# Spectral filter beside an MLP: the forward width transform as ten times 64 on VectorE and five full blocks on TensorE, filter loads behind the tile transposes, new instruction order

## The chip, the cores and the metric

The kernel runs on one core of one Trainium2 chip. The metric is device time in microseconds (us). Five engines work side by side, each with an instruction stream of its own: TensorE (PE, matmuls), VectorE (DVE), ScalarE (ACT), GpSimd (POOL) and SyncE (SP, which here issues most DMAs). They meet only at semaphores.

## The reference

The sum of three things: the input, a two-dimensional spectral filter of its normalized rows, and a two-layer MLP of the same normalized rows. S is 2048, D is 640, F is 1536, all in bf16.

```python
def _A_ref(x, w_r, w_i):
    B, S, D = x.shape
    X = jnp.fft.rfft2(x.astype(jnp.float32), axes=(-2, -1))
    X = X * (w_r + 1j * w_i)
    return jnp.fft.irfft2(X, s=(S, D), axes=(-2, -1)).astype(jnp.bfloat16)

def _B_ref(x, w1, b1, w2, b2):
    h = _gelu(jnp.einsum("bsd,df->bsf", x, w1) + b1)
    return jnp.einsum("bsf,fd->bsd", h, w2) + b2

xn = _layernorm(x, axis=-1)
return x + _A_ref(xn, A_w_r, A_w_i) + _B_ref(xn, B_w1, B_b1, B_w2, B_b2)
```

## The kernel before

**Tiles.** The 2048 rows are 16 tiles c of 128 rows (row 16p + c lies on partition p); two tiles that follow each other are a pair. Each tile is loaded into `X`, its statistics are taken on DVE (L670, L672), the inverse deviation on POOL (L674, `rstd`), and the normalized tile is written to `T` on DVE (L695).

**The MLP.** Normalized tiles are transposed into `xnT`: tiles 0 to 3 on PE (L714), 4 to 15 by DMA transposes that SP issues (L702). The first layer multiplies `xnT` with the first weights (in the profile `ps<-xnT,W`), ACT applies the gelu into `gT` (L774), and the second layer multiplies `gT` with the second weights (`ps<-W,gT`: a 512-column and a 128-column matmul, a pair, for each 128 of F and each tile). For the tiles in `KEEP` the second layer is finished early, and DVE adds it to a float32 tile (L948) that already holds the second bias (ACT, L924) and the input x, which a POOL DMA accumulates onto it (L942).

**The spectral branch.** Real transforms, in steps:
- *Folding.* DVE folds a tile's 640 columns twice by symmetry (L726: sums and differences of columns d and 639 - d; L730: the same again), a pair at a time. Four sets of 160 columns come out: four blocks of 128, and one block of 128 made of the four leftovers of 32.
- *First height step.* Each of the five blocks is multiplied with `gtab` (L737), ten matmuls a pair, and copied to `XV` (L742).
- *Forward width transform.* `XV` is multiplied with `etab` (L798). For the tiles of a group, each of four sets takes one matmul with 128 rows and one more with the 32 leftover rows (`width`, L778, gives the two lists; `five` starts and stops the sums). ACT and DVE copy the result into `Xb` (L805), two instructions for a group.
- *Second height step* on `mtab` (L816), four 32 x 32 blocks side by side; the result goes to `Y`.
- *Filter.* DVE multiplies with the filter `Wf` (L841) and adds up (L845) into `Z`.
- *Back.* `ntab` (L850), copies (L861), DMA transposes into `XV` (L866), then `getab` (L888), unfolding on DVE (L896, L901) and `htab` (L954), which adds into the PSUM tile of the MLP's second layer. DVE adds x and the bias (L957), and SP stores (L960).

**What sets the order.** `ORDER` (L158) fixes by numbers which operation follows which on each engine; an engine takes its list strictly from the front. `Sched` puts the semaphore waits where data or a buffer's reuse demands them. PE's list mixes spectral steps with matmuls of the MLP, which need nothing from the spectral branch and fill the time. The queue on SP is such a list too: a transpose that waits for DVE holds all loads behind it.

In the profile most helpers' instructions carry the helper's line: matmuls L550, copies L561 on ACT and L562 on DVE, loads L545.

Of the kernel before, what the change touches and what calls it, by code (L numbers as in the profile page):

```python
# [13 lines left out]
D = 640  # L14
# [13 lines left out]
def _tables():  # L28
# [22 lines left out]
    T["E"] = np.concatenate([e[:128] for e in E] + [np.concatenate([e[128:] for e in E])], axis=1)  # L51
# [50 lines left out]
def dve_us(n, rate=1.0):  # L102
    return 0.066 + n / 960.0 / rate
# [20 lines left out]
class Pool:  # L124
# [52 lines left out]
466 460 463 744 454 448 451 760 457 584 735 769 672 611 647 646 682 683 719 755""",  # L177
    "dve": """0 58 57 59 61 62 63 115 116 121 120 66 65 125 67 70 69 137 71 127 126 140 128 130 131 129 144 143 74 76 73 77 75 78
# [12 lines left out]
LAND = {8: 3.13, 13: 3.63, 14: 5.8, 15: 8.08, 16: 9.04, 18: 11.01, 19: 10.03, 20: 14.89, 21: 11.84, 22: 12.65, 23: 17.41, 26: 18.61, 27: 15.54, 28: 19.46, 30: 16.42}  # L191
LATE = {17: 0.5, 24: 0.4, 25: 0.7, 29: 2.0, 31: 1.0, 33: 0.5, 34: 1.6, 35: 1.4, 37: 1.4, 38: 0.4, 39: 1.7, 40: 2.3, 41: 1.7, 42: 0.2, 43: 0.4, 44: 2.5, 45: 0.4, 46: 2.2, 47: 0.9, 48: 1.6, 49: 2.9, 50: 0.3, 51: 1.2, 52: 2.5, 155: 0.3, 168: 0.9, 179: 1.0, 181: 1.0, 192: 0.6, 205: 1.0, 219: 0.7, 591: 1.1}
# [277 lines left out]
def bass_parallel_sum__spectral_gfnet__dense_activation_gelu__prompt_kernel(  # L470
# [21 lines left out]
    with ExitStack() as es:  # L492
# [14 lines left out]
        etab = sb("etab", [128, 800])  # L507
# [25 lines left out]
        XN, X1, XF = 0, 4 * D, 6 * D  # L533
# [7 lines left out]
        p_xn, p_x1, p_xf, p_xb, p_y, p_t, p_z, p_u = Pool(2), Pool(1), Pool(2), Pool(2), Pool(2), Pool(2), Pool(2), Pool(3)  # L541
# [42 lines left out]
        B_g, B_e, B_m, B_n, B_ge, B_h, B_w2 = [Buf(x) for x in ("g", "e", "m", "n", "i", "h", "w2")]  # L584
# [45 lines left out]
        def load_w2(h, **kw):  # L630
            load(W2[:, 3 * h:3 * h + 3, :], w2v[:, 3 * h:3 * h + 3, :], B_w2, (24, 1280), **kw)
# [12 lines left out]
        load(etab[:], const["E"], B_e, (8, 1600), gate=turned[3])  # L644
# [19 lines left out]
        for c0, n in [(c, 1) for c in range(4)] + [(c, 2) for c in range(4, 16, 2)]:  # L664
# [12 lines left out]
        for pair in range(8):  # L677
            xn, x1, xf = Buf(f"xn{pair}", p_xn), Buf(f"xe{pair}", p_x1), Buf(f"xf{pair}", p_xf)

            def xnv(n, o, dims, xn=xn):  # L680
                return view(TT, XN + xn.slot * 2 * D + n * D + o, dims)

            def x1v(o, dims, x1=x1):
                return view(TT, X1 + x1.slot * 2 * D + o, dims)

            def xfv(o, dims, xf=xf):
                return view(TT, XF + xf.slot * 2 * D + o, dims)
            for n in range(2):
                c = 2 * pair + n
                pr = 100 - c / 2  # L690
                B_xn = Buf(f"xn_{c}")
                cuts = (0, 256, D) if not c else (0, D)
                B_xs = [Buf(f"xn_{c}") for _ in cuts[2:]] + [B_xn]
                for d0, d1, bx in zip(cuts, cuts[1:], B_xs):
                    o = K.op([("dve", 0.066 + (d1 - d0) / 1980.0)], pr, lambda e, _, c=c, n=n, xnv=xnv, d0=d0, d1=d1: e.tensor_scalar(  # L695
# [304 lines left out]
```

## Time and profile before

| what | us |
|---|---|
| median of 3 runs | 146.87 |
| lowest and highest | 146.20 and 147.34 |
| span of the profiled execution, first to last instruction | 144.9 |
| first `gtab` run, first `etab` run, first `getab` run start | 15.3, 43.6, 110.1 |
| PE, DVE, ACT busy | 141.2, 112.2, 79.5 |

The profiled execution's own time outside its span is not recorded; the span stands 2.0 us below the median. In a group of the profile, the columns are line, engine, operation, what is written from what, shape and count; then busy us and the mean of one in ns; then the idle time of the engine before them and what ended it. A timeline row is start and length in us, engine, line, operation, count, and in brackets the idle time before it with what ended it. A row of the busy time by stretch gives the stretch, its length, the busy us of PE, PE's weight loads, DVE, ACT and POOL with their counts, the granted clock of PE, the share of the DMA engines and GB/s.

### The profile page before, as it was taken

How to read it: one execution, taken by the hardware profiler on the slowest of the kernel's cores; microseconds unless marked ns; L12 is line 12 of the kernel's file. 1: busy time of each engine (PE TensorE's matmuls, PEld its weight loads, DVE VectorE, ACT ScalarE, POOL GpSimd, SP SyncE). 2: the span in 40 equal slices, each digit the busy share in tenths (PEclk: the TensorE clock that was granted, in tenths of full speed). 3: DMA queues.
4: the chain of work that ended last, by engine and by line, in shares of the span. 5: the costliest groups of instructions: out<-in, count | busy, mean ns of one | idle time of the engine just before them, and what ended most of it. 6: DMA issues, size and time to landing. Idle time of an engine off the chain costs nothing.

```text
span 144.9 us, 4085 instructions
## 1 busy us (share of the span) xinstructions
PE 141.2 (97%) x1720; PEld 90.6 (63%) x1720; DVE 112.2 (77%) x235; ACT 79.5 (55%) x145; POOL 23.8 (16%) x40
## 2 busy tenths in 40 slices
PE   7899999999999999999999999999999999999994
PEld 7799998987455464457554645554446666656573
DVE  1999999999843459799866967992432998998984
ACT  3219999999989668762455633216376755201000
POOL 2331302206100018220200120000054700000000
DMA  4998998987999736948767561362459895103225
GB/s 117 340 410 321 339 164 255 160 146 202 212 301 168 186 59 129 241 104 170 153 179 127 59 144 42 46 142 59 91 112 216 180 209 187 52 5 136 93 106 165
DMA packets 30841, 23.63 MB, mean 163 GB/s; under 512 B 20456, under 2 KB 26856, under 8 KB 30696
## 3 DMA queue, kind: packets, MB, share of 16 engines
q1 hardware_dynamic: 28432, 17.81, 50.5%
q0 software_dynamic: 2368, 5.57, 17.7%
q8 instruction: 13, 0.21, 0.6%
q14 instruction: 4, 0.03, 0.1%
q10 hardware_dynamic: 24, 0.00, 0.0%
HBM read 13.54 MB, written 2.62 MB: 112 GB/s over the span
## 4 chain that ended last, share of the span: by engine, by line
PE 94%; DMA 2%; DVE 2%; issue 0%; ACT 0%
PE ps L550 94%; DMA X<-in_A_x_dram 2%; DVE stats L670 1%; PE ps L714 1%; DVE mv L672 0%; ACT xnT L561 0%; DVE W L957 0%; DVE T L695 0%
## 5 line engine op out<-in xcount | busy, mean ns | idle before, releaser
L550 PE MATMUL ps<-W,gT 128*128 128x512 bf16 (+3 forms) x396 | 58.7, 295 | 0.0
L550 PE MATMUL ps<-xnT,W 128*128 128x256 bf16 (+2 forms) x384 | 58.4, 300 | 0.1
L550 PEld LDWEIGHTS ps<-W,gT 128*128 128x128 bf16 x396 | 30.3, 98 | 23.5 <-issue 1.6
L550 PEld LDWEIGHTS ps<-xnT,W 128*128 128x128 bf16 x384 | 33.3, 98 | 15.7 <-issue 1.6
L774 ACT ACTIVATE gT<-ps,b1col 128x256 bf16<-128x256 f32 (+1 forms) x72 | 35.4, 558 | 6.9 <-PE ps L550 6.5
L670 DVE BATCH_NORM_STATS2 stats<-X 128x6 f32<-128x320 bf16 x32 | 13.9, 476 | 2.1 <-DMA X<-in_A_x_dram 2.1
L561 ACT ACTIVATE Wf<-ps 128x960 bf16<-128x960 f32 (+1 forms) x8 | 7.0, 901 | 13.5 <-PE ps L550 13.5
L942 POOL DMA_DIRECT2D X<-in_A_x_dram x8 | 7.1, 1100 | 39.7 <-DMA Wf<-in_A_w_r_dram 17.1
L841 DVE TENSOR_TENSOR T<-Y,Wf 128x1288 bf16<-128x1288 bf16 x16 | 12.7, 826 | 0.0
L942 POOL DMA_DIRECT2D xnT<-in_A_x_dram x8 | 7.6, 1193 | 25.1 <-ACT xnT L924 25.1
L674 POOL TENSOR_TENSOR rstd<-mv,mhalf 128x2 f32<-128x2 f32 (+1 forms) x10 | 7.1, 714 | 26.6 <-DVE mv L672 26.4
L562 DVE CAST Y<-ps 128x644 bf16<-128x644 f32 x8 | 6.5, 828 | 5.5 <-PE ps L550 5.5
L561 ACT ACTIVATE Xb<-ps 128x960 bf16<-128x960 f32 (+1 forms) x7 | 6.0, 857 | 7.3 <-PE ps L550 7.3
L561 ACT ACTIVATE XV<-ps 128x1280 bf16<-128x1280 f32 (+3 forms) x10 | 9.5, 963 | 0.7 <-PE ps L550 0.7
L562 DVE CAST Xb<-ps 128x960 bf16<-128x960 f32 (+1 forms) x5 | 5.5, 1092 | 4.3 <-PE ps L550 4.2
L730 DVE TENSOR_TENSOR T<-T 128x512 bf16<-128x512 bf16 (+1 forms) x32 | 8.5, 312 | 0.0
L695 DVE TENSOR_SCALAR T<-X,mv,rstd 128x640 bf16<-128x640 bf16 (+2 forms) x17 | 7.1, 430 | 0.9 <-POOL rstd L674 0.6
L896 DVE TENSOR_TENSOR Wf<-Wf 128x960 bf16<-128x960 bf16 (+1 forms) x12 | 7.0, 597 | 0.5 <-ACT Wf L561 0.3
L957 DVE TENSOR_TENSOR W<-ps,X 128x640 bf16<-128x640 f32 x8 | 6.5, 820 | 1.1 <-PE ps L550 1.1
L561 ACT ACTIVATE U<-ps 128x512 bf16<-128x512 f32 (+1 forms) x10 | 3.8, 434 | 6.2 <-PE ps L550 6.2
L845 DVE TENSOR_TENSOR Z<-T 128x644 bf16<-128x644 bf16 x16 | 7.2, 489 | 0.1
L957 DVE TENSOR_TENSOR W<-ps,xnT 128x640 bf16<-128x640 f32 (+2 forms) x10 | 6.7, 686 | 0.7 <-PE ps L550 0.7
(55 smaller groups left out, 135.4 us busy)
## 6 DMA issues: line engine op xcount, KB each, us to landing
X<-in_A_x_dram POOLq DMA_DIRECT2D x8, 320.0 KB, 5.2
xnT<-in_A_x_dram POOLq DMA_DIRECT2D x8, 320.0 KB, 5.1
out_dram<-W SPq DMA_DIRECT2D x15, 160.0 KB, 1.8
X<-in_A_x_dram SPq DMA_DIRECT2D x7, 320.0 KB, 6.7
W<-in_B_w_dram SPq DMA_DIRECT2D x5, 384.0 KB, 5.2
W<-in_B_w_dram SPq DMA_DIRECT2D x4, 480.0 KB, 7.2
Wf<-in_A_w_i_dram SPq DMA_DIRECT2D x6, 160.5 KB, 5.4
Wf<-in_A_w_r_dram SPq DMA_DIRECT2D x6, 160.5 KB, 4.0
```

The lines of the kernel that those rows point to most:

```text
L550: ins = e.matmul(o_, lhsT=lw, rhs=rh, start=st, stop=sp_, skip_group_check=True)
L561: return e.activation(dst(), src(), ACT.Copy, scale=scale)
L562: return e.tensor_copy(dst(), src())
L670: st_op[c] = K.op([("dve", 0.393)], pr, lambda e, _, c=c, h=h: e.bn_stats(stats[:, c, 6 * h:6 * h + 6], view(X, c * D + H2 * h, [[1, H2]]) ...
L674: K.op([("pool", 0.65)], 500, lambda e, _, a=a, b=b: e.tensor_tensor(out=rstd[:, a:b], in0=mv[:, a:b, 1], in1=mhalf[:, a:b], op=ALU.pow), ...
L695: o = K.op([("dve", 0.066 + (d1 - d0) / 1980.0)], pr, lambda e, _, c=c, n=n, xnv=xnv, d0=d0, d1=d1: e.tensor_scalar(out=xnv(n, d0, [[1, d1 ...
L730: ring_ops.append(K.op([("dve", dve_us(4 * w, 2))], pr, lambda e, _, op=op, x1v=x1v, xfv=xfv, o_=o_, o0=o0, o1=o1, w=w: e.tensor_tensor(ou ...
L774: K.op([("act", act_us(128 * nt, 1))], pr + PRIO["gelu"] + GP[bi], lambda e, _, c0=c0, nt=nt, fc=fc, hps=hps, at=at: e.activation(gT[:, fc ...
L841: filt_ops.append(K.op([("dve", dve_us(4 * KP, 2))], pr, lambda e, _, k=k, Y=Y, TB=TB, pair=pair: e.tensor_tensor(out=view(TT, TB.slot * 8 ...
L845: K.op([("dve", dve_us(2 * KP, 2))], pr, lambda e, _, TB=TB, Z=Z, r=r, op=op: e.tensor_tensor(out=view(Zb, Z.slot * 4 * KP + r * KP, [[2 * ...
L942: xo_ops[c] = K.op([("pool", 0.9)], 51 - c / 20, lambda e, _, c=c, xov=xov: e.dma_start(xov(0, D), xv[:, c, :], accum_op=ALU.add), reads=[ ...
L957: K.op([("dve", dve_us(w))], 95, lambda e, _, os_=os_, fps=fps, o0=o0, w=w, xov=xov, base=base: e.tensor_tensor(out=view(W1, OST + os_.slo ...
```

## The change

The forward width transform is cut in another way. 640 is ten times 64: column d is written as 64j + r, and a ten-point real transform over j is made on DVE, four tiles (a quad) at a time, with fourteen instructions: two and three-way sums and differences of columns 320 apart, then the five-point sums with their constants, three of them `scalar_tensor_tensor` (multiply by a constant and add) and one multiplication by a constant. Each tile then has five blocks of 128 columns, which go through `gtab` as before. The `etab` step needs one matmul of 128 rows and 128 columns for each block, and no leftover rows: 80 matmuls in place of 128. The copies into `Xb` then have to spread the results ten or five columns apart, and are four, or three, or two instructions in place of one.

```diff
-        for pair in range(8):
-            xn, x1, xf = Buf(f"xn{pair}", p_xn), Buf(f"xe{pair}", p_x1), Buf(f"xf{pair}", p_xf)
+        for quad in range(4):
+            xn, x1, tm, xf = Buf(f"xn{quad}", p_xn), Buf(f"xe{quad}", p_x1), Buf(f"xs{quad}", p_tm), Buf(f"xf{quad}", p_xf)
...
-            for k, op in enumerate((ALU.add, ALU.subtract)):
-                K.op([("dve", dve_us(640, 2))], pr, lambda e, _, k=k, op=op, xnv=xnv, x1v=x1v: e.tensor_tensor(
...
+            def tt(op, out, in0, in1):
+                return lambda e, _: e.tensor_tensor(out=out(), in0=in0(), in1=in1(), op=op)
+
+            def stt(c_, out, in0, in1):
+                return lambda e, _: e.scalar_tensor_tensor(out=out(), in0=in0(), scalar=c_, in1=in1(), op0=ALU.mult, op1=ALU.add)
...
+            b0 = fold("fp", dve_us(4 * H2, 2), tt(ALU.add, lambda: uv_(0, [[D, 4], [1, H2]]), ...
+            b1 = fold("fm", dve_us(768, 2), tt(ALU.subtract, ...
+            b2 = fold("fn", dve_us(512, 2), tt(ALU.subtract, ...
+            b3 = fold("fs", dve_us(1024, 2), tt(ALU.add, ...
+            b4 = fold("fd", dve_us(1024, 2), tt(ALU.subtract, ...
+            b5 = fold("gs", dve_us(512, 2), tt(ALU.add, ...
+            fold("i1", dve_us(512), stt(kap, ...
+            b6 = fold("gd", dve_us(512, 2), tt(ALU.subtract, ...
+            b7 = fold("ge", dve_us(512), stt(-0.25, ...
+            fold("i2", dve_us(512), stt(-kap, ...
+            b8 = fold("gk", dve_us(512, 2), lambda e, _: e.tensor_scalar(...
+            fold("zr", dve_us(512, 2), tt(ALU.add, ...
+            fold("zp", dve_us(512, 2), tt(ALU.add, ...
+            fold("zm", dve_us(512, 2), tt(ALU.subtract, ...
...
-            pb_ops.append(pe(five_segs(n), PRIO["pb"] - c0 / 10, lambda c0=c0, n=n, bps=bps: five(
-                bps.slot, n, lambda i, g, p0, k: part(XV, p0, k, 2048 * g + 128 * (c0 + i), [[1, 128]]), etab),
+            pb_ops.append(pe([("128", 5 * n * mm_us(128))], PRIO["pb"] - c0 / 10, lambda c0=c0, n=n, bps=bps: [
+                (psb(bps.slot + (g if g < 4 else i), [[1, 128]], 128 * i if g < 4 else 384), view(XV, 2048 * g + 128 * (c0 + i), [[1, 128]]), etab[:, 128 * g:128 * g + 128], True, True)
+                for g in range(5) for i in range(n)],
...
+                    for h in range(2):
+                        k0, dk = (2 * m + 1, 1) if not h else (9 - 2 * m, -1)
+                        ins = copy(lambda: view(xb3, xb.slot * 6 * KP + k0, [[KP, 2 * n], [dk, 2], [10, 32]]),
+                                   lambda: psb(bps.slot + 2 * m, [[64, 2 * n], [512, 2], [1, 32]], 32 * h))(e, name)
+                    for i in range(2 * m, 2 * m + na):
+                        ins = copy(lambda: view(xb3, xb.slot * 6 * KP + 2 * KP * i, [[KP + 5, 2], [5, 64]]),
+                                   lambda: psb(bps.slot + i, [[64, 2], [1, 64]], 384))(e, name)
```

Around it: `rstd` is made tile by tile for eight tiles in place of four; each quarter of the second weights `W2` has a wait of its own; early PSUM tiles of the MLP may use all eight banks (`ZONE["early"]`); the loads that accumulate x no longer wait for the filter loads, and those of the tiles in `SOON` not for the tile transposes either.

```diff
+SOON = (0, 2, 3, 5)
...
-            load(W2[:, 3 * h:3 * h + 3, :], w2v[:, 3 * h:3 * h + 3, :], B_w2, (24, 1280), **kw)
+            load(W2[:, 3 * h:3 * h + 3, :], w2v[:, 3 * h:3 * h + 3, :], B_w2[h], (24, 1280), **kw)
...
-            xo_ops[c].gate += [WL[-1], TD[15]]
-            xo_ops[c].deps += WL + list(TD.values())
+            xo_ops[c].deps += list(TD.values()) if c not in SOON else []
...
 ORDER = {
-    "sp": """8 13 14 17 15 16 19 18 21 22 20 27 30 23 26 28 153 155 166 168 31 32 35 46 48 37 179 181 192 194 38 39 41 34 44 33
+    "sp": """8 13 14 17 15 16 19 18 21 22 27 23 157 159 161 163 28 26 20 31 29 185 187 189 191 30 32 33 35 34 213 217 219 215 46 48
```

All five lists of `ORDER` are new. Rows of the order give the line, the operation, what is written from what, and the written shape; line numbers of the changed kernel are its own.

On DVE, the folding in the first third of the program, before (tile statistics L670 and L672, normalization L695, folds L726 and L730):

```order
L695 TENSOR_SCALAR T<-X,mv,rstd 128x640
L730 TENSOR_TENSOR T<-T 128x2x2x128 x2
L730 TENSOR_TENSOR T<-T 128x2x2x32 x2
L726 TENSOR_TENSOR T<-T 128x2x320 x2
L670 BN_STATS stats<-X 128x6 x4
L672 BN_AGGR mv<-stats 128x2 x2
```

and now the fold of the first quad (sums L752, multiply and add L755, multiplication L770; normalization is L712):

```order
L712 TENSOR_SCALAR T<-X,mv,rstd 128x640 x4
L752 TENSOR_TENSOR T<-Z 128x1024
L752 TENSOR_TENSOR U2<-Z 128x1024
L752 TENSOR_TENSOR T<-T 128x512
L755 SCALAR_TENSOR_TENSOR Y<-U2 128x8x64
L752 TENSOR_TENSOR T<-T 128x8x64
L755 SCALAR_TENSOR_TENSOR Y<-U2 128x8x64
L755 SCALAR_TENSOR_TENSOR T<-T,Z 128x8x64
L770 TENSOR_SCALAR T<-T 128x8x64
L752 TENSOR_TENSOR Y<-T,Z 128x512
L752 TENSOR_TENSOR Y<-T 128x8x64 x2
```

Where a few short folds stood between statistics, eleven of a quad's fourteen instructions now stand in a row, writing the five blocks to `Y`.

On PE, from the last `gtab` runs to the first `etab` runs, before (W1 and W2 are the two weights):

```order
L550 MATMUL ps<-gtab,T 128x64x2 x10
L550 MATMUL ps<-xnT,W1 128x512 x8
L550 MATMUL ps<-gtab,T 128x64x2 x10
L550 MATMUL ps<-xnT,W1 128x512 x6
L550 MATMUL ps<-etab,XV 128x160 x24
L550 MATMUL ps<-xnT,W1 128x512 x9
L550 MATMUL ps<-etab,XV 128x160 x16
```

and now, up to the last `gtab` runs, behind which six pairs on `W2` and then the first `etab` row stand:

```order
L572 MATMUL ps<-gtab,Y 128x64x2 x20
L572 MATMUL ps<-xnT,W1 128x512 x10
L572 MATMUL ps<-xnT,W1 128x256 x5
L572 MATMUL ps<-xnT,W1 128x512 x5
L572 MATMUL ps<-gtab,Y 128x64x2 x20
L572 MATMUL ps<-W2,gT 128x512
L572 MATMUL ps<-W2,gT 128x128
```

The `gtab` runs come by two pairs at once, and second-layer pairs on `W2` now stand ahead of the width transform, thirty of them in all where none stood.

On SP, the queue from the first tile transposes to the third set, before:

```order
L702 DMA_TRANSPOSE xnT<-T 128x5x128 x4
L545 DMA X<-in_A_x_dram 128x1280
L545 DMA W2<-in_B_w2_dram 128x3x640
L545 DMA mtab<-c_M 128x256
L545 DMA Wf<-in_A_w_i_dram 16x16x321 x2
L545 DMA Wf<-in_A_w_r_dram 16x5136
L702 DMA_TRANSPOSE xnT<-T 128x5x128 x4
L545 DMA Wf<-in_A_w_i_dram 16x5136
L545 DMA Wf<-in_A_w_r_dram 16x5136 x2
L545 DMA etab<-c_E 128x800
```

and now:

```order
L719 DMA_TRANSPOSE xnT<-T 128x5x128 x4
L567 DMA X<-in_A_x_dram 128x1280
L567 DMA W2<-in_B_w2_dram 128x3x640
L567 DMA gtab<-c_G 128x2048
L567 DMA X<-in_A_x_dram 128x1280
L567 DMA W2<-in_B_w2_dram 128x3x640
L719 DMA_TRANSPOSE xnT<-T 128x5x128 x4
L567 DMA b2bc<-in_B_b2_dram 128x640
L567 DMA W2<-in_B_w2_dram 128x3x640 x2
L567 DMA mtab<-c_M 128x256
L567 DMA etab<-c_E 128x640
L719 DMA_TRANSPOSE xnT<-T 128x5x128 x4
```

`gtab`, the second bias and two loads of x moved behind the first transposes, and all sixteen SP loads of `Wf` behind the third set.

More of the change, by code (lines that the diff above doesn't have):

```diff
@@ L663, in bass_parallel_sum__spectral_gfnet__dense_activation_gelu__prompt_kernel @@
         mv_ops, st_op = [], {}
[L664 removed]
+        for c0, n in [(c, 1) for c in range(8)] + [(c, 2) for c in range(8, 16, 2)]:
             pr = 100 - c0 / 2
@@ new lines, in bass_parallel_sum__spectral_gfnet__dense_activation_gelu__prompt_kernel @@
+            fold("zp", dve_us(512, 2), tt(ALU.add, lambda: view(Yb, 0, row), lambda: view(TT, SM + 64, row), lambda: view(TT, SM, row)), [b7, b8], [tm, xf])
+            fold("zm", dve_us(512, 2), tt(ALU.subtract, lambda: view(Yb, 1024, row), lambda: view(TT, SM + 64, row), lambda: view(TT, SM, row)), [b7, b8], [tm, xf])
+            for pair in (2 * quad, 2 * quad + 1):
+                aps = Buf(f"aps{pair}", psum, 3, ZONE["aps"])
+                for n in range(2):
+                    c = 2 * pair + n
+                    o = pe([("128", 5 * mm_us(128))], pr - pair, lambda c=c, n=n, aps=aps: [
+                        (psb(aps.slot, [[4, 64], [1, 2]], 256 * j + 2 * n), view(Yb, (1152 + 256 * (c % 4), 256 * (c % 4), 128 + 256 * (c % 4), 1024 + 256 * (c % 4), 2048 + 128 * (c % 4))[j], [[1, 128]]), gtab[:, 128 * c:128 * c + 128], True, True) for j in range(5)],
+                        reads=[xf, B_g], writes=[aps])
+                    ring_ops.append(o)
+                    a_ops.append(o)
+                for js in [[int(j) for j in g] for g in XASPLIT[pair].split()]:
+                    K.op([("dve", dve_us(256 * len(js))), ("act", act_us(256 * len(js)))], pr,
+                         copy(lambda pair=pair, js=js: view(XV, 2048 * js[0] + 4 * pair, [[2048, len(js)], [32, 64], [1, 4]]),
+                              lambda aps=aps, js=js: psb(aps.slot, [[256, len(js)], [4, 64], [1, 4]], 256 * js[0])),
+                         reads=[aps], writes=[B_xa[pair]])
@@ L937, in second @@
                             for fc in range(f0, f0 + 3) for a, b in sums(o0, w)],
-                            reads=[B_w2] + [B_gT[c, fc] for fc in range(f0, f0 + 3)], writes=[fps], gate=part_ + gate)]
+                            reads=[B_w2[f0 // 3]] + [B_gT[c, fc] for fc in range(f0, f0 + 3)], writes=[fps], gate=part_ + gate)]
                     return part_
```

127 lines of the change are left out of this document (74 added, 53 removed), and 36 rows, old and new, of the table ORDER.

## The prediction

> **What bounds the kernel now.** I read the page first, then the busy time by stretch, then the timelines of TensorE (PE) and VectorE (DVE), the by-form groups, and last the queues.
>
> ```profile
> span 144.9 us, 4085 instructions
> PE 141.2 (97%) x1720; PEld 90.6 (63%) x1720; DVE 112.2 (77%) x235; ACT 79.5 (55%) x145; POOL 23.8 (16%) x40
> PE ps L550 94%; DMA X<-in_A_x_dram 2%; DVE stats L670 1%; PE ps L714 1%; DVE mv L672 0%; ACT xnT L561 0%; DVE W L957 0%; DVE T L695 0%
> ```
> ```profile
> 10.00:41.00 31.00, 31.00 (x306) 25.75 (x304) 29.37 (x96) 29.62 (x62) 6.08 (x9) 1.00 1.01 235
> 41.00:66.00 25.00, 25.00 (x377) 13.10 (x376) 16.48 (x26) 18.38 (x31) 5.35 (x6) 1.00 0.76 162
> 66.00:110.00 44.00, 44.00 (x616) 22.94 (x614) 30.53 (x48) 19.37 (x36) 5.48 (x6) 1.00 0.56 111
> ```
>
> The chain that ended last is 94% matmuls, and the PE column of the stretches (first after the length) is full from 10 to 110 us at a granted clock of 1.00. So the kernel lasts as long as PE's work, and time is won only by taking work from PE without making it wait. The DVE column (third) says where that is dangerous: 29.37 of 31 us up to 41, then 16.48 of 25 and 30.53 of 44. DVE has no room in the first stretch, where the change puts its new work, and room behind it. The last column but one is the DMA share: 1.01, then 0.76.
>
> **What PE saves.** The forward width transform is six runs on `etab`: four of 24 matmuls, two of 16.
>
> ```profile
> L550 PE MATMUL ps<-etab,XV 128*128 128x160 bf16 x64 | 5.4, 233 | 0.0
> L550 PE MATMUL ps<-etab,XV 32*128 32x160 bf16 x64 | 2.2, 232 | 0.0
> ```
> ```profile
> 22.03 6.18 PE L550 MATMUL ps<-xnT,W 128*128 128x256 bf16 x55
> 28.05 0.72 PE L550 MATMUL ps<-gtab,T 128*128 128x128 bf16 x10
> 28.61 3.44 PE L550 MATMUL ps<-xnT,W 128*128 128x256 bf16 x30
> 43.63 1.31 PE L550 MATMUL ps<-etab,XV 128*128 128x160 bf16 x24
> 44.88 2.12 PE L550 MATMUL ps<-xnT,W 128*128 128x512 bf16 x9
> 46.83 0.97 PE L550 MATMUL ps<-etab,XV 128*128 128x160 bf16 x16
> 47.73 1.25 PE L550 MATMUL ps<-xnT,W 128*128 128x512 bf16 x5
> ...
> 90.90 5.88 PE L550 MATMUL ps<-W,gT 128*128 128x512 bf16 x42
> 96.71 0.49 PE L550 MATMUL ps<-Z,ntab 32*32 32x320 bf16 x32
> ...
> 103.09 5.14 PE L550 MATMUL ps<-xnT,W 128*128 128x512 bf16 x23
> 108.07 1.79 PE L550 MATMUL ps<-W,gT 128*128 128x512 bf16 x12
> ```
>
> Matmuls overlap, so I price them from one start to the next. A run of 24 takes 44.88 - 43.63 = 1.25 us, one of 16 takes 0.90: together 4 x 1.25 + 2 x 0.90 = 6.8 us. The new transform has 80 matmuls of 128 columns with 128 rows of weights, the shape of the `gtab` run: 10 in 28.61 - 28.05 = 0.56 us, so 4.5 us. PE saves 2.3 us. All other matmuls keep their number and shape.
>
> The Trainium skill, TensorEngine Tiling (Array Packing), section Theoretical Speedup, says that matmuls on 32 rows may run up to four at once. By that the 64 leftover matmuls would weigh as 16 whole ones and the saving be 80 x (0.070 - 0.056) = 1.1 us, an estimate that makes the sum below -0.1 in place of -1.3. The trace is against it: of the 1.25 us of a run, twelve whole matmuls at 160/128 of 0.056 us explain 0.84, and the twelve leftover ones take the other 0.41, twice what the rule gives.
>
> **What DVE pays.** DVE is priced in the same way.
>
> ```profile
> L726 DVE TENSOR_TENSOR T<-T 128x640 bf16<-128x640 bf16 x16 | 7.1, 477 | 0.1
> L730 DVE TENSOR_TENSOR T<-T 128x512 bf16<-128x512 bf16 x16 | 6.3, 413 | 0.0
> L730 DVE TENSOR_TENSOR T<-T 128x128 bf16<-128x128 bf16 x16 | 3.0, 212 | 0.0
> L562 DVE CAST T<-ps 128x512 bf16<-128x512 f32 x3 | 2.1, 692 | 3.8 <-PE ps L550 3.8
> ```
> ```profile
> 28.60 1.01 DVE L730 TENSOR_TENSOR T<-T 128x512 bf16<-128x512 bf16 x4
> 29.52 0.49 DVE L670 BATCH_NORM_STATS2 stats<-X 128x6 f32<-128x320 bf16 x1
> 38.84 0.56 DVE L730 TENSOR_TENSOR T<-T 128x512 bf16<-128x512 bf16 x2
> 40.26 0.43 DVE L562 CAST XV<-ps 128x256 bf16<-128x256 f32 x1 [0.86 <-PE ps L550]
> 40.60 0.55 DVE L730 TENSOR_TENSOR T<-T 128x128 bf16<-128x128 bf16 x2
> 55.03 2.31 DVE L841 TENSOR_TENSOR T<-Y,Wf 128x1288 bf16<-128x1288 bf16 x3
> 57.25 1.70 DVE L845 TENSOR_TENSOR Z<-T 128x644 bf16<-128x644 bf16 x4
> 58.87 0.82 DVE L948 TENSOR_TENSOR X<-ps,X 128x640 f32<-128x640 f32 x1
> ```
>
> Three products of 1288 take 2.22 us and four sums of 644 take 1.62: 0.74 and 0.405 each, so 0.52 ns an element and 0.07 us apiece. Means of one are some 0.08 us longer, which the next instruction hides unless it waits. Before, two rows of tiles take 2 x 0.40 + 2 x 0.33 + 2 x 0.13 = 1.73 us: 13.9 for eight pairs. Now four tiles take sums and differences of 1280, 768, 512 (0.73 + 0.47 + 0.33), two of 1024 (1.20), six 512-element steps at 0.33 (2.0) and three `scalar_tensor_tensor` of 512. The trace has none of these. Bounds: 0.33, the plain sum of 512, and 0.61, the 692 ns conversion less the 0.08 that hides. I take 0.60, one element per tick, since multiply and add are two operations. That makes 6.5 us: 26.1 for four, and 12.2 more than before. At the lower bound it is 3.2 less. That pieces of 64 elements lose the rate is excluded by the 128x128 row, made of pieces of 32: 212 ns.
>
> This does not hide: DVE was full there. The old folds end at 40.60 + 0.55 = 41.15; without the 0.86 us wait and the 0.34 us copy in front of them, 39.95. Add 12.2 and two of the L948 additions, now ahead of the last fold (1.6): 53.75. Instructions that wait for the one before cost 0.08 more: none to 56 of them, so 0 to 4.5 us. The order puts others between most; I take three in each fold, 1.0: the last fold ends at 54.7, bounds 50.5 and 58.2.
>
> PE fills the time. Ahead of the first `etab` run it now has 15 more L550 matmuls of 256 (0.109 each by the 55-run), 16 more of 512 (0.217 by the 23-run) and 30 pairs on `W2` (0.277 by the 42-run): 1.6 + 3.5 + 8.3 = 13.4 us, so the run stands at 57.0. Six pairs (1.7) and the last two `gtab` runs (1.1) come just before, so PE asks for the last fold at 54.2. It waits 0.5 us. Behind the last `gtab` run DVE has two copies of 512 and one of 256 from PSUM, 1.6 to 1.8 us, against 1.7 us of PE cover: 0.2 more. Above the bound of 58.2 PE would wait 4.0.
>
> The `gtab` table, issued at 5.8 before, now stands on SP behind four tile transposes and two loads, at some 22; the other tables and `W2` quarters behind it are asked for later and have more cover. On POOL two filter loads move ahead of the last two `rstd` steps, which DVE asks for some ten of its instructions later: nothing.
>
> ```profile
> GB/s 117 340 410 321 339 164 255 160 146 202 212 301 168 186 59 129 241 104 170 153 179 127 59 144 42 46 142 59 91 112 216 180 209 187 52 5 136 93 106 165
> gtab<-c_G SPq DMA_DIRECT2D x1, 512.0 KB, 8.8
> ```
>
> PE first asks for it 28.4 us of its work ahead of `etab`, at 28.6. With the 8.8 us of before it lands at 30.8; but then over 2 MB stood ahead, and now 800 KB, which with its own 512 KB take 3.9 us at 340 GB/s (the second slice): 26 and its start-up. I take no wait; at the other end PE loses 2.2, in place of the 0.5 for the last fold and not beside it.
>
> The spreading copies grow from 12 to 40: some 28 x 0.07 = 2 us more over DVE and ACT, in stretches where both have room (16.48 and 18.38 of 25); nothing on PE.
>
> **What moves behind.** The first `etab` run comes 13.4 us later, the last stage only 1.6 earlier on PE, so the chain through filter and inverse transform is squeezed into what were DVE's idle parts. Its sums there fit. Its end:
>
> ```profile
> 99.51 0.49 PE L550 MATMUL ps<-Z,ntab 32*32 32x320 bf16 x32
> 110.13 0.72 PE L550 MATMUL ps<-getab,XV 128*128 128x160 bf16 x8
> ```
> ```profile
> 107.77 0.63 DVE L562 COPY Y<-XV 128x512 bf16<-128x512 bf16 x1 [2.19 <-DMA XV<-gtab]
> ```
>
> From the last `ntab` run to the end of the last copy it took 108.4 - 99.5 = 8.9 us, and PE had 10.6 of cover. Now it has the run (0.4) and 30 pairs, 8.7. PE waits 0.2 to 0.5, since ACT puts an addition of its own into the chain; I take 0.3.
>
> The sum: -2.3 + 0.5 + 0.2 + 0.3 = -1.3 us on a span of 144.9, which stands 2.0 below the median of the runs, 146.87. On that: **145.6 us**. Within 1% (145.4 to 148.3) is about what a measurement cannot tell from no change.
>
> **Rivals.** *The whole saving stays.* The fold ends by 54.2, say because `scalar_tensor_tensor` runs at 0.33, and the end is covered: 146.87 - 2.3 = 144.6. For it: the order leaves PE no hole if DVE keeps step. Against: no row has these instructions. 0.24.
>
> *Filter loads too late; slower.* All sixteen on the SP queue now stand behind the last tile transposes, which wait for DVE.
>
> ```profile
> 39.71 5.91 SPq L702 DMA_TRANSPOSE xnT<-T  x4
> 45.66 0.65 SPq L545 DMA_DIRECT2D Wf<-in_A_w_r_dram  x1
> 47.63 1.92 SPq L545 DMA_DIRECT2D Wf<-in_A_w_r_dram  x3
> ...
> 53.81 3.62 POOL L942 DMA_DIRECT2D X<-in_A_x_dram  x4 [17.14 <-DMA Wf<-in_A_w_r_dram]
> ```
>
> By the prices above 14 to 11 us of DVE work follow the last four normalizations up to the end of the fold: they are done at 41 to 43.5. Four transposes take the queue 5.9: loads from 46.8, 0.65 each, to 57.2. Before, the last of six came 53.8 - 49.5 = 4.3 after its issue: 61.5. At the pace of those six, 8.1 us for six, sixteen land at 68.5, and up to six accumulating loads of x, freed from waiting for the filter, run beside them. DVE wants the filter at some 65 (5.9 us of PE's work behind the first `etab` run, and a copy), PE the first `ntab` run at about 72 (14.2 us behind it), with 5.4 us of DVE work between. It decides when the last lands after 67: at 70.5 PE waits 3.5 and the time is 149.1. DMA share 0.76 speaks for the early end. 0.17.
>
> *The saving is eaten.* Folds at the middle of the upper half of their bound, 56.5, cost 1.8 more: 147.4; `gtab` at 30.8 gives 147.3. A second way there: the spreading copies write 2 bytes every 20. If each took twice its 0.3 to 0.45 us, the two in the first run's chain would hold PE 0.8 us, and the time would be 146.4. No row writes so; I give that 0.05 of 0.17. The Trainium skill, SBUF — State Buffer, section Door 1: The DMA port swizzle, speaks for it: accesses that each fall in a new 16-byte line pay a penalty by it.
>
> **Numbers.** Forecast case 0.42 (144.9 to 146.3), of which 0.17 lies under 145.4; whole saving 0.24; eaten 0.17; late filter 0.17. Faster 0.41, same 0.42, slower 0.17. The range leaves out most of the late filter: 144.3 to 148.4.
>
> **What would show it.** `etab` at some 0.056 us a matmul; the last fold near 54.7 and PE idle there under 1 us; the three-operand steps near 0.69 us; no DVE wait for Wf. It is wrong if PE is idle by more than 2 us in one place, or if the `etab` matmuls keep 0.07 us.

## The result, and the profile after

The changed kernel takes 173.08 us (median of four runs, 171.55 to 174.94) where the kernel before takes 146.7 (now four runs too): the ratio is 1.175, with a 95% interval of 1.168 to 1.183. The forecast was 145.6, with a range up to 148.4. It is slower by 26.4 us, and the profiled execution lasts 172.2 us against 144.9. Times here and below are medians of all runs of a kernel, while ratios and their intervals leave out the runs that took over 1.5% longer than its fastest one, so the two need not divide out (e8 and e11 above all).

From the page of the changed kernel: the span, the busy time of the engines, the PE and clock rows in forty slices, and the chain that ended last, by engine.

```profile
span 172.2 us, 4011 instructions
PE 149.6 (87%) x1672; PEld 91.7 (53%) x1672; DVE 128.8 (75%) x246; ACT 108.2 (63%) x170; POOL 24.9 (14%) x42
PE   7899999999999938942993979379979999999995
PEclk9999999999999996995699699956999999999999
PE 51%; ACT 21%; DMA 13%; DVE 6%; SPq 5%; issue 3%; DVEq 0%
```

PE was 97% busy and held 94% of the chain that ended last; now it is 87% busy and holds 51%, and ACT has 21%. The PE row has holes from the fifteenth slice on, that is from 60 us, where the new width transform starts. The clock row falls to 5 and 6 near them, so the matmuls that follow a hole also run slower. PE should have had 141.2 - 2.3 = 138.9 us of work and shows 149.6; the other part of the loss is idle time.

The busy time by stretch, with the granted clock in the last column but two:

```profile
57.00:66.00 9.00, 6.08 (x56) 3.82 (x54) 6.41 (x8) 7.30 (x9) 0.00 (x0) 0.91 0.75 129
66.00:110.00 44.00, 33.16 (x483) 14.73 (x481) 32.55 (x47) 37.51 (x52) 2.62 (x3) 0.86 0.32 62
110.00:140.00 30.00, 25.68 (x340) 12.49 (x341) 13.61 (x23) 18.01 (x29) 6.59 (x10) 0.89 0.52 111
```

In these 83 us PE is busy for 64.9. ACT is busy for 37.5 of 44 us in the middle stretch, where it had 19.4 before. The timeline of PE in these stretches, with the wait ahead of a row in brackets:

```profile
58.80 1.00 PE L572 MATMUL ps<-etab,XV 128*128 128x128 bf16 x15
...
64.18 1.03 PE L572 MATMUL ps<-etab,XV 128*128 128x128 bf16 x10 [2.92 <-ACT Xb L583]
...
80.86 0.77 PE L572 MATMUL ps<-Xb,mtab 32*32 32x322 bf16 x32 [5.57 <-ACT Xb L583]
...
94.45 1.16 PE L572 MATMUL ps<-etab,XV 128*128 128x128 bf16 x15 [2.87 <-ACT Xb L583]
...
112.81 0.77 PE L572 MATMUL ps<-Xb,mtab 32*32 32x322 bf16 x32 [3.49 <-ACT Xb L583]
```

Every long wait is for a spreading copy into Xb: the `mtab` runs wait for their operand, and an `etab` run waits until the copies of the run before have freed its PSUM banks. What these copies cost stands in the groups by form (busy time, then the mean of one in ns):

```profile
L583 ACT ACTIVATE Xb<-ps 128x384 bf16<-128x384 f32 x10 | 18.1, 2060 | 0.9 <-PE ps L572 0.8
L583 ACT ACTIVATE Xb<-ps 128x128 bf16<-128x128 f32 x11 | 7.0, 785 | 0.0
L584 DVE CAST Xb<-ps 128x384 bf16<-128x384 f32 x6 | 10.7, 1976 | 1.1 <-PE ps L572 1.1
L755 DVE SCALAR_TENSOR_TENSOR Y<-U 128x512 bf16<-128x512 bf16 x8 | 5.4, 682 | 0.0
```

A copy of 384 elements takes 2.06 us on ACT and 1.98 on DVE, where the prediction had 0.3 to 0.45 for the spreading copies. It writes 2 bytes every 20. That the two engines get in each other's way does not explain it: from 76.4 to 80.1 us ACT copied while DVE did nothing, and its two copies of 384 took 2.03 and 2.21 us. The last row, the three-operand step, is what the prediction took (0.60 and the 0.08 that hides).

### The profile page after: what moved, and what is told of

Its sections match the earlier page's. It is cut to its first block, busy times and chain, and to the rows that moved or that the text cites. A ratio compares the mean times of both kernels' runs of the same rounds, so it can differ in the third digit from the quotient of the medians.

```text
span 172.2 us, 4011 instructions
## 1 busy us (share of the span) xinstructions
PE 149.6 (87%) x1672; PEld 91.7 (53%) x1672; DVE 128.8 (75%) x246; ACT 108.2 (63%) x170; POOL 24.9 (14%) x42
## 4 chain that ended last, share of the span: by engine, by line
PE 51%; ACT 21%; DMA 13%; DVE 6%; SPq 5%; issue 3%; DVEq 0%
PE ps L572 51%; ACT Xb L583 15%; DMA gtab<-c_G 5%; DMA X<-in_A_x_dram 4%; DMA XV<-U 4%; DVE stats L693 4%; SPq L567 3%; SPq L918 3%; ACT Y L583 1%; ACT gT L816 1%; ACT U L583 1%; DVE T L712 1%; ACT X L976 1%; ACT xnT L976 1%; ACT T L583 1%
## 5 line engine op out<-in xcount | busy, mean ns | idle before, releaser
L572 PE MATMUL ps<-W,gT 128*128 128x512 bf16 (+3 forms) x396 | 61.8, 306 | 0.1
L572 PE MATMUL ps<-xnT,W 128*128 128x256 bf16 (+2 forms) x384 | 60.5, 309 | 0.5 <-DMA W<-in_B_w_dram 0.5
L583 ACT ACTIVATE Xb<-ps 128x128 bf16<-128x128 f32 (+2 forms) x27 | 28.9, 1421 | 2.5 <-PE ps L572 2.4
L584 DVE CAST Xb<-ps 128x384 bf16<-128x384 f32 (+2 forms) x13 | 14.9, 1400 | 2.6 <-PE ps L572 2.6
L572 PE MATMUL ps<-Xb,mtab 32*32 32x322 bf16 x256 | 5.0, 379 | 9.7 <-ACT Xb L583 9.1
L697 POOL TENSOR_TENSOR rstd<-mv,mhalf 128x1 f32<-128x1 f32 (+1 forms) x12 | 8.3, 700 | 29.1 <-DVE mv L695 29.1
L572 PE MATMUL ps<-etab,XV 128*128 128x128 bf16 x80 | 5.9, 229 | 6.0 <-ACT Xb L583 5.8
L583 ACT ACTIVATE Y<-ps 128x644 bf16<-128x644 f32 x9 | 6.3, 706 | 5.7 <-PE ps L572 5.7
L1000 DVE TENSOR_TENSOR X<-ps,X 128x640 f32<-128x640 f32 x8 | 6.6, 830 | 3.3 <-PE ps L572 3.3
L572 PEld LDWEIGHTS ps<-etab,XV 128*128 128x128 bf16 x80 | 4.8, 101 | 8.0 <-ACT Xb L583 6.6
```

The costliest lines, as they stand in the source:

```text
L572: ins = e.matmul(o_, lhsT=lw, rhs=rh, start=st, stop=sp_, skip_group_check=True)
L583: return e.activation(dst(), src(), ACT.Copy, scale=scale)
L584: return e.tensor_copy(dst(), src())
L697: K.op([("pool", 0.65)], 500, lambda e, _, a=a, b=b: e.tensor_tensor(out=rstd[:, a:b], in0=mv[:, a:b, 1], in1=mhalf[:, a:b], op=ALU.pow), ...
L1000: kept_ops.append(K.op([("dve", dve_us(D))], 30, lambda e, _, kps=kps, xov=xov: e.tensor_tensor(out=xov(0, D), in0=psb(kps.slot, [[1, D]]) ...
```

## The experiments

The theory that the trace suggests: a copy that scatters its writes is slow, and this alone makes the kernel slow. Its rivals: the reads from PSUM are slow; or the copies are slow, but the new order holds PE anyway. In a kernel with a line less, the line numbers are smaller by one.

### e1: the same copies, unbroken writes

```diff
-  copy(lambda: view(xb3, xb.slot * 6 * KP + k0, [[KP, 2 * n], [dk, 2], [10, 32]]),
+  copy(lambda: view(xb3, xb.slot * 6 * KP + 64 * (2 * m + h + 1), [[KP, 2 * n], [32, 2], [1, 32]]),
        lambda: psb(bps.slot + 2 * m, [[64, 2 * n], [512, 2], [1, 32]], 32 * h))
...
-  copy(lambda: view(xb3, xb.slot * 6 * KP + 2 * KP * i, [[KP + 5, 2], [5, 64]]),
+  copy(lambda: view(xb3, xb.slot * 6 * KP + 2 * KP * i, [[KP, 2], [1, 64]]),
        lambda: psb(bps.slot + i, [[64, 2], [1, 64]], 384))
```

> The changed kernel, with the 40 spreading copies writing rows of 64 and 128 neighbouring elements instead of 2 bytes every 20 or 10; same instructions, same sizes, same reads from PSUM, same order (the columns of Xb then stand in another order, so the output is not the reference's). Theory A, the scattered writes are what costs: a copy of 128x384 falls from 2.06 us on ACT and 1.98 on DVE to 0.45 to 0.50, PE is no longer idle behind the etab runs, the granted clock stays at 1.00, and the time is 147.1 us (the forecast of 145.6 plus 1.5 that the changed kernel's trace loses ahead of the first etab run), 145.5 to 149. Rival B, the reads cost (32-element runs of two PSUM banks): the copies keep about 2 us and the time stays near 173. Rival C, the copies are slow but something else holds PE too: copies of 0.5 us and a time above 155.

Measured: 150.07 us, ratio 1.022 (1.019 to 1.026); that is 1.1 us above the range expected. Of the 26.4 us, 173.08 - 150.07 = 23.0 are gone with the order of the writes alone. The page's head, the middle stretch and the copies by form:

```profile
span 147.8 us, 3993 instructions
PE 139.9 (95%) x1654; PEld 89.5 (61%) x1672; DVE 118.6 (80%) x246; ACT 88.0 (60%) x170; POOL 25.0 (17%) x42
```
```profile
66.00:110.00 44.00, 41.75 (x691) 20.97 (x698) 34.54 (x61) 33.29 (x70) 6.17 (x7) 1.00 0.73 125
```
```profile
L583 ACT ACTIVATE Xb<-ps 128x384 bf16<-128x384 f32 x10 | 4.4, 494 | 0.7 <-PE ps L572 0.6
L583 ACT ACTIVATE Xb<-ps 128x128 bf16<-128x128 f32 x11 | 2.6, 297 | 0.0
```

The copies fall from 2060 to 494 ns with the same reads, so the reads were not what cost. The clock is at 1.00 again. The two spans differ by 24.4 us: 9.7 is PE's busy time (149.6 - 139.9), put down here to the slow clock, and 14.7 is idle time (18 of e1's matmul records are missing, some 0.085 us each, an estimate, so up to 1.5 us of the first belongs to the second). Some 3 us remain to the kernel before, so the rival that the order also costs something is right in a small part.

### e2: pairs of neighbours

```diff
-  [[KP, 2 * n], [dk, 2], [10, 32]]      [[64, 2 * n], [512, 2], [1, 32]]
+  [[KP, 2 * n], [10, 32], [dk, 2]]      [[64, 2 * n], [1, 32], [512, 2]]
```

The left column is what is written, the right one what is read.

> The changed kernel, with the inner two loops of the 24 main spreading copies exchanged, so that they write two neighbours (4 bytes) every 20 in place of 2 bytes; the 16 copies of the last block keep 2 bytes every 10. Same output, same count. Theory A with a price for each separate run written (4.2 to 4.4 ns): 192 runs in place of 384, so a 128x384 copy takes 0.95 to 1.05 us, the 128x128 ones stay at 0.70 to 0.79, and the time falls by a part, to 153 to 163. If the price is for each element that is not in an unbroken row, the copies stay at 2 us and the time at 173. Rival B (reads): reads now alternate between two banks for each element, so no faster than now, 173.

Measured: 155.08 us, ratio 1.056 (1.053 to 1.060). A 128x384 copy took 972 ns on ACT, as expected:

```profile
L583 ACT ACTIVATE Xb<-ps 128x384 bf16<-128x384 f32 x10 | 8.1, 972 | 0.7 <-PE ps L572 0.6
```

The output is as before, so exchanging two loops of the copy gains 18.0 us of the 26.4.

### e3: the price against the step

> A measuring kernel: the changed kernel with another step between the written elements in each of the six groups (20 bytes with n=2, 2 bytes, 4 bytes, 8 bytes and 16 bytes with n=3, pairs of 4 bytes every 20 with n=2); the output is not the reference's. What counts is the duration of a copy by group. Theory A1, each write that does not touch its neighbour pays the same, some 4.2 ns: about 0.47 us at 2 bytes and about 2 us at 4, 8, 16 and 20 alike. Theory A2, a new line of 16 bytes pays (the Trainium skill, SBUF — State Buffer, section Door 1: The DMA port swizzle, names such a line): 0.5 at 4 bytes, at most 1.2 at 8, and 2 us only at 16 and 20. Rival B (reads): 2 us in every group.

One look, with the durations of the two main copies of one group on ACT (shortest, median, longest in ns); the groups write every 2, 4, 8 and 16 bytes:

```profile
L583 ACT ACTIVATE Xb<-ps x2: 486/489/492, 60.2 to 60.6; 128x384 bf16<-128x384 f32 x2
L583 ACT ACTIVATE Xb<-ps x2: 635/640/646, 69.9 to 70.3; 128x384 bf16<-128x384 f32 x2
L583 ACT ACTIVATE Xb<-ps x2: 1068/1117/1166, 84.8 to 85.6; 128x384 bf16<-128x384 f32 x2
L583 ACT ACTIVATE Xb<-ps x2: 1878/2039/2200, 79.9 to 81.3; 128x384 bf16<-128x384 f32 x2
```

And from the changed kernel itself, every 20 bytes:

```profile
L583 ACT ACTIVATE Xb<-ps x2: 1877/2038/2200, 90.1 to 91.5; 128x384 bf16<-128x384 f32 x2
```

489, 640, 1117, 2039, 2038: the time grows with the step, by nearly a factor of two from 4 to 8 and from 8 to 16 bytes, and not beyond. A price for each write apart (A1) would give 2 us from 4 bytes on; it is the number of 16-byte lines that counts (A2). From 8 to 16 bytes 192 more lines cost 2039 - 1117 = 922 ns, 4.8 ns a line. That price is not one constant: from 2 to 4 bytes 48 more lines cost 151 ns, 3.1 each, and the small copies (2 bytes every 10, so 80 lines in place of 16) went from 297 to 785 ns, 7.6 each. Why is open. The Trainium skill, SBUF — State Buffer, section Door 1: The DMA port swizzle, names lines of 16 bytes, and the knee at 16 agrees; it also says that two accesses to a line are enough for the full rate, and here two to a line (8 bytes) take 1117 ns against 489. The measurement decides. DVE pays the same (1976 ns against ACT's 2060 in the changed kernel).

### e4 and e5: the kernel before, with scattered writes

```diff
-  view(xb3, xb.slot * 6 * KP + v * (KP + 1), [[2 * KP, n], [2, Q4], [1, 2]])   psb(..., [[Q4, n], [1, Q4], [512, 2]])
+  view(xb3, xb.slot * 6 * KP + v * (KP + 1), [[2 * KP, n], [1, 2], [2, Q4]])   psb(..., [[Q4, n], [512, 2], [1, Q4]])
```

for every 4 bytes, and for every 16:

```diff
+  view(xb3, xb.slot * 6 * KP + v * n * 320, [[4, 2], [1, 4], [8, 40 * n]])   psb(..., [[512, 2], [40 * n, 4], [1, 40 * n]])
```

> The kernel before, with its 12 copies into Xb writing every second element (2 bytes every 4) of the same rows instead of neighbours; nothing else changed (the columns of Xb stand in another order, so the output is not the reference's). Theory A1, each separate write pays about 4.2 ns: a 128x960 copy goes from 0.97 to about 4.2 us on ACT and from 1.16 to about 4.2 on DVE, 128x640 to 2.9, PE waits behind the etab runs, and the kernel is slower by 5 to 15%: 154 to 169. Theory A2, the 16-byte line pays, and eight elements share one here: copies of 1.0 to 1.2 us and 146.9 within 1%. Rival B (reads): this reads PSUM in unbroken rows, so no slower than before.

> The kernel before, with its 12 copies into Xb writing every eighth element (2 bytes every 16) of an unbroken piece of the same size; same reads, same counts, and the columns of Xb stand in another order, so the output is not the reference's. Theory A2 with the price of the strides run (0.9 us for 384 at 8 bytes, 1.7 at 16, so 4.4 ns for each new 16-byte line): a 128x960 copy goes from 0.97 us on ACT and 1.16 on DVE to 4.2 on both, 128x640 to 2.8, PE stands behind the etab runs, the granted clock falls in places, and the time is 152 to 168. Rival: the stall comes from the order of the changed kernel and the old order has cover for longer copies: copies of 4.2 us and a time within 2% of 146.7.

The 4-byte edit only exchanges two loops, so its columns of Xb stand where they stood and the output is right, other than expected. Both edits also change the order of the reads, from alternating between two PSUM banks to unbroken rows; so the pair to compare is these two kernels with each other.

Measured: every 4 bytes 146.75 us, ratio 1.000 (0.999 to 1.002); every 16 bytes 168.57 us, just above the upper end expected, ratio 1.144 (1.137 to 1.151). The copies by form, of the kernel before, of the 4-byte kernel, then of the 16-byte one, and the first `etab` runs of the last:

```profile
L561 ACT ACTIVATE Xb<-ps 128x960 bf16<-128x960 f32 x4 | 3.9, 972 | 5.3 <-PE ps L550 5.2
```
```profile
L561 ACT ACTIVATE Xb<-ps 128x960 bf16<-128x960 f32 x4 | 5.0, 1257 | 5.0 <-PE ps L550 5.0
```
```profile
L561 ACT ACTIVATE Xb<-ps 128x960 bf16<-128x960 f32 x4 | 17.7, 4426 | 5.9 <-PE ps L550 5.8
L562 DVE CAST Xb<-ps 128x960 bf16<-128x960 f32 x4 | 17.6, 4410 | 3.5 <-PE ps L550 3.5
```
```profile
44.46 1.31 PE L550 MATMUL ps<-etab,XV 128*128 128x160 bf16 x24
45.71 2.12 PE L550 MATMUL ps<-xnT,W 128*128 128x512 bf16 x9
50.38 0.96 PE L550 MATMUL ps<-etab,XV 128*128 128x160 bf16 x16 [2.56 <-ACT Xb L561]
```

720 more lines cost 4426 - 1257 = 3169 ns, 4.4 ns a line. With the copies into Xb alone touched, the old kernel loses 14% at the same runs and in the same way. So the old order has no cover for such copies either: the scattered writes are enough for a loss of this size.

### e6, e7, e8: what else the new order costs

All three have e1's unbroken writes. e6 puts the `gtab` load (number 20) ahead of the first tile transposes on SP; e7 takes the wait for eight transposes of XV from the loads of x for tiles 9 and 11 and puts these ahead of an xnT load on POOL; e8 does both.

```diff
-  SP    21 22 27 23 157 159 161 163 28 26 20 31 29
+  SP    21 22 27 23 20 157 159 161 163 28 26 31 29
-  POOL  699 627 647 719 709 736
+  POOL  699 627 709 719 647 736
-  WAVE = (0, 3, 0, 0, 2, 0, 0, 4, 0, 2, 0, 2, 4, 2, 2, 3)
+  WAVE = (0, 3, 0, 0, 2, 0, 0, 4, 0, 0, 0, 0, 4, 2, 2, 3)
```

> The changed kernel with unbroken writes (as e1), and the gtab load put back ahead of the first tile transposes on SP. Theory: the table then lands by 20, PE's wait of 0.78 us at 29.6 is gone, but the last fold still ends at 55.5 and PE asks for it some 0.3 before that, so 0.5 of the 0.78 is kept: span 147.3, ratio to before 1.018 to 1.020 in place of 1.0221. Rival: PE's wait only moves to the fold, span 147.8, 1.022; or the table takes bandwidth from W1 and x and the start loses more, span over 148.

> The changed kernel with unbroken writes (as e1), and the two accumulating loads of x for tiles 9 and 11 freed of their wait for eight transposes of XV and put ahead of the load of xnT on POOL. Theory: the addition that waits 1.35 us for x at 100.3 runs at once, PE's waits of 0.48 and 0.28 us at 101.6 and 102.5 are gone: span 146.8 to 147.1, ratio 1.015 to 1.018. Rival: the loads run beside the transposes of XV and make them later, or the next copy is late anyway: span 147.6 or more.

> Both of the last two together with the unbroken writes. Theory: the gains add, span 146.3 to 146.6, ratio 1.011 to 1.015, still not below the kernel before, since some 2 us of waits of 0.2 to 0.4 us for copies out of PSUM between 80 and 115 stay. Rival, the forecast's own sum: without these waits 143.6 to 144.5 and faster than before.

Measured: e6 148.38 us, ratio 1.010 (1.006 to 1.014), more than expected; e7 150.73, 1.027 (1.024 to 1.031), the rival; e8 149.07, 1.014 (1.010 to 1.018), in the range given for the ratio, but its profiled span of 147.4 us misses the 146.3 to 146.6: the gains don't add, and what there is comes from e6's edit alone. What PE waited for in e1 and in e6, a part of each list (total, times, longest):

```profile
PE ps L572 <- DMA gtab<-c_G: 0.8, 1, 0.8
PE ps L572 <- DVE Y L584: 0.3, 2, 0.2
PE ps L572 <- DVE X L999: 0.3, 1, 0.3
```
```profile
PE ps L572 <- DVE U L584: 1.1, 1, 1.1
...
PE ps L572 <- DVE X L999: 0.9, 1, 0.9
PE ps L572 <- DVE Y L584: 0.3, 2, 0.2
```

The wait for `gtab` is gone. In the profiled execution of e6, which took 149.02 us, two waits behind 100 us had grown in its place: an addition that waits for x, and a copy into U that waits until the transposes of XV have read an older U.

### e10 and e12: the two late waits

e10 is e6 with the 16 accumulating loads of x cut to 64 columns. e12 has a fourth buffer for U besides, in the upper part of `gtab`'s memory.

```diff
-  e.dma_start(xov(0, D), xv[:, c, :], accum_op=ALU.add)
+  e.dma_start(xov(0, 64), xv[:, c, 0:64], accum_op=ALU.add)
...
-  p_u = Pool(3)
+  p_u = Pool(4)
```

> The kernel of e6 (unbroken writes, gtab early) with the 16 accumulating loads of x cut to the first 64 of 640 columns; the other columns of x are left out of the last sum, and the columns of Xb stand in another order as in e6. Theory: behind 90 us PE waits for transfers that get in each other's way, the loads of x (7 us to landing) and the transposes of XV (5.0 us in place of 2.7): with small loads the wait of 1.4 us of a DVE addition for x and the 2.0 us of a copy for XV are gone, PE's 0.9 at 100.3 and 1.1 at 103.0 with them, span 145.5 to 146.2, ratio 0.995 to 1.003. Rival: the copies out of PSUM on DVE and ACT hold PE anyway, span over 147.2, ratio 1.007 to 1.013.

> The kernel of e10 (unbroken writes, gtab early, accumulating loads of x cut to 64 columns) with the fourth buffer for U; the other columns of x are left out of the last sum, and the columns of Xb stand in another order. Theory: PE's wait of 1.18 us at 102.8 goes and nothing takes its place: span 146.5 or less in place of 147.7, ratio 1.004 to 1.007. Rival: the chain behind it is as late as before and PE waits ahead of the getab runs: span 147.4 to 147.9, ratio 1.012 to 1.015.

Measured: e10 148.70 us, ratio 1.014 (1.011 to 1.016), so small loads alone gain nothing: PE's wait of 1.1 us at 103.0 ahead of an `ntab` run stayed, and the theory that transfers only get in each other's way fell. e12 147.15 us, ratio 1.005 (1.002 to 1.007), as expected: the buffer was what held it. What PE still waited for in e12 behind its first 10 us, in the list of waits:

```profile
PE ps L571 <- ACT Y L582: 0.5, 1, 0.5
PE ps L571 <- DVE Y L583: 0.3, 2, 0.2
```

### e9 and e11: a version with the right output

Here Xb takes whole blocks of 32 neighbours (block r from column 33 r), and the 16 copies from PSUM to Y put the coefficients back in order: they read PSUM with a step of 132 bytes and write unbroken rows. e9 has e6's `gtab`, e11 the fourth buffer for U too.

```diff
-  view(xb3, xb.slot * 6 * KP + k0, [[KP, 2 * n], [dk, 2], [10, 32]])
+  view(xb3, xb.slot * 6 * KX + 33 * k0, [[KX, 2 * n], [33 * dk, 2], [1, 32]])
...
-  copy(view(Yb, Y.slot * 4 * KP + r * KP, [[2 * KP, 2], [1, KP]]), psb(cps.slot + 2 * pp, [[512, 2], [1, KP]]))
+  copy(view(Yb, Y.slot * 4 * KX + r * KX, [[2 * KX, 2], [10, 33], [1, 10]]), psb(cps.slot + 2 * pp, [[512, 2], [1, 33], [33, 10]]))
```

> A version with the right output: each spreading copy writes whole blocks of 32 neighbours into Xb (block r at column 33 r), and the order of the coefficients is restored by the 16 copies from PSUM to Y, which now read PSUM with a step of 33 floats (132 bytes) and write unbroken rows; gtab stands ahead of the first transposes as in e6. Theory A2, only the line written counts: copies into Xb of 0.5 to 0.6 us, copies to Y at 0.71 to 0.85 us as they were, and the time of e6 plus at most 1%: 148.4 to 150, ratio 1.010 to 1.022; it repairs the change but does not beat the kernel before. Rival: scattered reads of PSUM cost as scattered writes do (the Trainium skill, SBUF — State Buffer, section Door 1: The DMA port swizzle, gives PSUM lines of 8 bytes): 660 elements at 4.4 ns make 2.9 us a copy, PE waits behind every mtab run, and the time is 160 to 175.

> The version of e9 with a fourth buffer for U (the upper part of gtab's memory), so that a copy out of an ntab run no longer has to wait until the transposes of XV have read an older one; same output as e9. Theory: in e6 and e10 DVE stood 2.0 to 2.3 us before such a copy at 101 to 103 and PE lost 1.1 to 1.2 us to it ahead of an ntab run; with the buffer this is gone and the rest stays: ratio to before 1.005 to 1.009 in place of 1.015, about 147.8 us. Rival: what ends the inverse stage is the chain of copies and transposes themselves, so PE waits as long a little later, ahead of the getab runs: ratio 1.012 to 1.018.

Measured: e9 148.98 us, ratio 1.015 (1.012 to 1.018), as expected; e11 149.11 us (147.44 to 150.69), ratio 1.012 (1.007 to 1.016). Whether the fourth buffer helps this version is not settled: the two intervals overlap, and that of e11 reaches into the range of its theory and of its rival. The copies by form, of the changed kernel (first row) and of e11:

```profile
L583 ACT ACTIVATE Y<-ps 128x644 bf16<-128x644 f32 x9 | 6.3, 706 | 5.7 <-PE ps L572 5.7
...
L583 ACT ACTIVATE Y<-ps 128x660 bf16<-128x660 f32 x9 | 6.4, 720 | 2.8 <-PE ps L572 2.8
L583 ACT ACTIVATE Xb<-ps 128x384 bf16<-128x384 f32 x10 | 4.4, 501 | 0.7 <-PE ps L572 0.6
L584 DVE CAST Y<-ps 128x660 bf16<-128x660 f32 x7 | 5.9, 844 | 2.1 <-PE ps L572 1.9
```

The copies to Y take 720 ns for 660 elements read in steps, where the changed kernel's take 706 for 644 read in rows: a scattered read of PSUM costs nothing here. So the same reordering, moved from the write of one copy to the read of the next, repairs, together with the early `gtab`, some 24 of the 26.4 us with the output unchanged. It does not beat the kernel before; no version of the changed kernel does.

## Why the prediction was wrong

**The step that failed** is the sentence on the spreading copies, "some 28 x 0.07 = 2 us more over DVE and ACT, in stretches where both have room (16.48 and 18.38 of 25); nothing on PE". It priced them as plain copies. The mechanism stood under the rivals ("the spreading copies write 2 bytes every 20"), but at twice the time of a copy, with 0.8 us for the first run only, and a chance of 0.05. Measured, a copy takes 2060 ns against 494 when its writes are unbroken, over four times, and the copies held PE for 2.9 to 5.6 us at four places, by the operand of the `mtab` runs and by the PSUM banks of the next `etab` run: the idle time of over 2 us in one place that the prediction named as the sign of its being wrong. Two things were missed. The page of before has no scattered write, and the price was bounded by a guessed factor and not from below and above; a bound of four times would have shown the danger. And the price was multiplied by two copies, where there are 24 main copies in six groups, and four of the six groups held PE.

**What the loss is made of**, against the forecast: 173.08 - 145.6 = 27.5 us. Scattered writes 23.0 (e1). The late `gtab` 1.7 (e6 against e1). The loads of x and the buffer of U 1.2 (e12 against e6). That leaves 147.15 - 145.6 = 1.5. Behind its first 10 us e12 has seven gaps of 0.1 to 0.5 us on PE, 1.3 in all, five of them ended by copies out of PSUM, the largest, 0.5, by a copy from XV to Y ahead of the first `getab` run; the forecast had 1.0 of waits in its sum, so these gaps do not explain all of the 1.5. The medians of the kernel before in these sets lie within 0.2 us of each other.

**The saving on `etab`** was right. From each start to the next, summed over PE's records, the runs on `etab` take 6.77 us before and 4.46 in e12: 2.3 as forecast, and the twelve leftover matmuls did weigh what the trace said. In the same sums the pairs on `W2` grow by 2.25 (55.53 against 53.28), of which 1.3 is idle time, since a wait counts to the pair ahead of it; the matmuls on W1 grow by 0.7. That is where the saving went in e12, whose span is 145.7 against 144.9; the growth that is not idle time was not traced.

**The folds** were right within a microsecond. The row of the last two steps of the last fold, and of the last `gtab` runs on PE, which did not wait for them, in the changed kernel:

```profile
54.77 0.76 DVE L752 TENSOR_TENSOR Y<-T 128x512 bf16<-128x512 bf16 x2
```
```profile
30.34 0.72 PE L572 MATMUL ps<-gtab,Y 128*128 128x128 bf16 x10 [0.60 <-DMA gtab<-c_G]
...
56.02 1.28 PE L572 MATMUL ps<-gtab,Y 128*128 128x128 bf16 x20
```

The last fold ends at 55.5 (forecast 54.7, bounds 50.5 and 58.2). PE came to it later than the forecast's 54.2, at 56.0, so the 0.5 did not fall due, and neither did the 0.2 behind it. Of these 1.8 us, 0.5 is a wait for W1 and 0.6 the wait for `gtab`; the rest was not traced.

**`gtab`** came late. The forecast took "26 and its start-up" from a rate of 340 GB/s; it landed at 30.2, after 8.3 us, close to the 8.8 that the row of before had. The other end of that bound, 30.8, was the better value.

**What moves behind** was wrong at "Its sums there fit". Sums of busy time did fit (34.5 of 44 us on DVE in e1), but the inverse stage ran into the three buffers of U, a resource that no sum of busy times shows. Its end cost 0.5 in e12, the upper end of what the forecast allowed (0.2 to 0.5).

**The late filter loads** did not hold anything: no wait is ended by a load of the filter, and the loads were issued from 48.6 to 59.9, against 46.8 to 57.2 in that rival.

## What to carry to other kernels

Look at what an access pattern writes and not only at how many elements: here each 16-byte line of SBUF that a copy on ACT touched anew cost 4.4 to 4.8 ns in the copies with most lines, so 2 bytes every 16 or 20 made a copy four times as long, on DVE too, while a read of PSUM in steps of 132 bytes was free. Where a permutation has to happen between PSUM and SBUF, try it on the read. And where an operation has no row in the trace, price it by a bound that could be true, and multiply it by all its places on a chain without slack, before giving it a small chance.

## What the runs showed of the hardware that was not expected

- Time of a copy of 384 elements from PSUM to SBUF against the step of its writes: 489 ns at 2 bytes, 640 at 4, 1117 at 8, 2039 at 16, 2038 at 20. ACT and DVE pay alike (4426 and 4410 ns for 960 lines).
- A wait of PE costs twice. In the changed kernel PE was idle from 75.3 to 80.9; within this wait, at 78.1, the granted clock fell to 0.50, where it stayed until 84.9, and the `mtab` run at 80.9 took 0.77 us, where the one at 68.5 took 0.50. There are four such stretches, from 64.5, 78.1, 95.2 and 112.2 us on, 20.5 us in all, each from 2.8 to 3.6 us after PE fell idle. PE is busy for 17.1 of them, so at half the clock they cost up to 8.6 us, of the 24.4 between the spans of the changed kernel and e1. The Trainium skill, TensorE: Matmul & The Clock Gate, section What's actually happening, gives a half-rate clock after an idle window of some 3.4 us. The half rate agrees. As a least length of the wait, 3.4 us does not: two of the four waits lasted only 2.9 us, and the clock fell all the same. The rows around the longest wait:

```profile
74.90:78.30 3.40, 0.39 (x2) 0.00 (x0) 0.61 (x2) 3.40 (x4) 0.00 (x0) 0.97 0.00 0
78.30:88.50 10.20, 7.64 (x146) 2.56 (x147) 5.22 (x9) 7.17 (x13) 0.00 (x0) 0.68 0.01 2
```
